# Down projection with stationary tokens, and a second filter step with products of 512: one change to a fused Hyena-filter and gated-MLP kernel

## The chip, the cores and the metric

The kernel runs on one core of one Trainium2 chip. The metric is the device time of one execution in microseconds (us). Engines are named as in the profile: PE is TensorE's matmul, PEld its weight load, DVE is VectorE, ACT is ScalarE, POOL is GpSimd.

## The reference

```python
# x, v: (4, 12480, 128); pos_emb: (12480, 64); w1: (64, 64); w2: (64, 128)
h_filt = (np.maximum(pos_emb @ w1, 0.0) @ w2) * np.exp(-0.01 * pos)[:, None]
u = x * v
L = 2 * S                                            # S = 12480
y = irfft(rfft(u, n=L, axis=1) * rfft(h_filt, n=L, axis=0), n=L, axis=1)[:, :S, :]
x2 = (x * y).reshape(B * S, D)                       # 49,920 tokens of 128
h = x2 @ w_in                                        # w_in: (128, 2048)
return (h * np.cos(h)) @ w_out                       # w_out: (2048, 128)
```

All of it is fp32.

## The kernel before

The long convolution is a Fourier transform in two steps, a product with the filter's transform, and an inverse in two steps, all as matmuls. The filter and batch 0 are transformed first; everything after that is the MLP with the convolution of the following batches fed into it in small pieces. The MLP takes the tokens in 98 tiles of up to 128 rows by 4 tokens (512 columns, one PSUM bank), and each tile has 16 steps, one per 128 hidden channels. A step is an up product, then k and f (which bring the argument of the cosine into the sine's range), the sine, the gate, and four steps later the down product. The down product kept the weights stationary, so its sums lay channel by token and were transposed back at the end of the tile:

```python
def moe_up(pool, n, c):
    ph = ps_h.tile([P, BANK], F32, name="ph")                  # 4 banks
    nc.tensor.matmul(ph[:, 0:m], w_in_sb[:, c * P:(c + 1) * P], ats[n][:, 0:m], ...)
    nc.scalar.activation(a[:, 0:m], ph[:, 0:m], AF.Identity, bias=quarter[:, 0:1], scale=INV_TWO_PI)
    nc.vector.tensor_scalar(out=k[:, 0:m], in0=a[:, 0:m], ...)              # k: round a
    nc.gpsimd.tensor_tensor(f[:, 0:m], a[:, 0:m], k[:, 0:m], op=ALU.subtract)
    # ... then in moe_act: cs = Sin(f) on ScalarE, gt = ph * cs on VectorE

def moe_down(n, c, gt):                                        # acc: 1 bank
    nc.tensor.matmul(accs[n][:, 0:m], w_out_sb[:, c, :], gt[:, 0:m],
                     start=(c == 0), stop=(c == NFC - 1))

def moe_evict(pool, n):
    nc.scalar.copy(out=ot[:, 0:m], in_=accs.pop(n)[:, 0:m])

def moe_back(pool, n, ot):
    for i in range(G):                                         # G = 4
        transpose(pt[0:m, i * D:(i + 1) * D], ot[:, i * m:(i + 1) * m], ident)
    nc.scalar.copy(out=ob[0:m, :, :].rearrange("p h n -> p (h n)"), in_=pt[0:m, :])
```

The second step of the transform is followed by the complex product with the filter. Each `yield` ends a turn: the program hands the engines back to the MLP there. A pair of rows has four turns in the time of 2.9 MLP steps, so a step is followed by one turn or by two.

```python
def f2_product(pool, ps, h, k1):
    for r, op in ((0, ALU.subtract), (1, ALU.add)):
        nc.vector.tensor_tensor(y[:, r], uu[:, 0], hh[:, r], op=ALU.mult)       # 256 columns
        yield
        nc.vector.tensor_tensor(t[:, r], uu[:, 1], hh[:, 1 - r], op=ALU.mult)   # 256 columns
        nc.gpsimd.tensor_tensor(y[:, r], y[:, r], t[:, r], op=op)
        yield
```

At the start, batch 0's x*v is made in 30 tiles of two halves, spread over two engines half by half, while the filter's two layers and its first step run:

```python
first_u = u_units(0, 3, slots[0:R, :, :, :],
                  lambda j, half: nc.vector if half and j % 3 and j < 18 else nc.gpsimd)
# the sums of a tile: add on GpSimd, subtract on VectorE
```

## Time and profile before

| | before |
|---|---|
| time, median of three runs | 3786.0 us (3785.1 to 3786.1) |
| first product of the second inverse step of batch 0 | 338.7 us |
| last down product starts | 3778.3 us |
| span of the profiled run | 3783.9 us |

The prediction below shows the stretches, TensorE's timeline and four groups of instructions.

The timeline of all engines at one change of tiles (start, duration, instruction, in brackets the idle time before it and its releaser):

```profile
1011.59 0.63 ACT L741 ACTIVATE cs<-f 128x512 f32<-128x512 f32 x1 [0.55 <-POOL f L736]
...
1012.13 0.57 ACT L758 COPY ot<-acc 128x512 f32<-128x512 f32 x1
...
1012.75 0.70 PE L752 MATMUL acc<-gt,w_out_sb 128*128 128x512 f32 x1 [0.28 <-ACT ot L758]
```

### The profile page before, as it was taken

The page shows a single profiled execution, that of the slowest core. Times are in us where ns is not written, and L with a number is a line of the kernel's source. Part 1 is how long each engine was busy: PE and PEld are TensorE (multiplying, and loading weights), DVE is VectorE, ACT ScalarE, POOL GpSimd, SP SyncE. Part 2 cuts the span into 40 slices and gives each one's busy share as a digit, 9 for nine tenths or more (in the row PEclk, how much of TensorE's full clock was granted, in tenths as well). Part 3 has the DMA queues.
Part 4 walks back from the last instruction along what each step waited for, and adds up shares of the span by engine and source line. Part 5 has one row for each costly group of instructions (what it writes and reads, how often), then busy time and mean ns, then how long its engine had stood idle before and what let it go on. Part 6 is the DMA issues. An engine that isn't in the chain of part 4 may idle for free.

```text
span 3783.9 us, 47244 instructions
## 1 busy us (share of the span) xinstructions
PE 3704.6 (98%) x13546; PEld 2108.5 (56%) x13546; DVE 2774.6 (73%) x5658; ACT 2525.1 (67%) x4683; POOL 2594.2 (69%) x2342
## 2 busy tenths in 40 slices
PE   8898999999999999999999999999999999999999
PEld 6777555655466555555565556555566544444444
DVE  8887887688866777788766786788765566666666
ACT  5756776766665557766655567666664677777777
POOL 7666886488854665688745664788644577777776
PEclk9999999999999999999999999999999999999999
DMA  6253542022202550122203540122105200000000
GB/s 166 70 178 100 151 148 60 16 72 78 75 18 66 177 162 27 32 78 77 60 18 109 173 127 18 52 78 76 41 12 167 87 20 21 17 20 20 17 22 14
DMA packets 209499, 276.14 MB, mean 73 GB/s; under 512 B 17111, under 2 KB 146535, under 8 KB 209111
## 3 DMA queue, kind: packets, MB, share of 16 engines
q1 hardware_dynamic: 209239, 273.12, 24.4%
q8 instruction: 109, 1.79, 0.2%
q14 instruction: 151, 1.24, 0.1%
HBM read 193.64 MB, written 79.42 MB: 72 GB/s over the span
## 4 chain that ended last, share of the span: by engine, by line
PE 84%; POOL 7%; DVE 4%; ACT 2%; issue 2%; DMA 1%; SPq 0%; POOLq 0%; DVEq 0%; ACTq 0%
PE ph L727 31%; PE acc L752 26%; PE cv L752 5%; PE cv L491 5%; PE cv L466 4%; POOL f L736 4%; PE cv L402 3%; PE cv L442 3%; PE ph L126 2%; PE ps L402 2%; PE ps L442 1%; DVE k L733 1%; POOL slots L461 1%; ACT cs L741 1%; POOL tm L295 1%
## 5 line engine op out<-in xcount | busy, mean ns | idle before, releaser
L736 POOL TENSOR_TENSOR f<-a,k 128x512 f32<-128x512 f32 (+1 forms) x1568 | 1988.6, 1268 | 1049.6 <-DVE k L733 1048.6
L727 PE MATMUL ph<-at,w_in_sb 128*128 128x512 f32 (+1 forms) x3136 | 1601.0, 592 | 5.3 <-DVE gt L743 4.7
L730 ACT ACTIVATE a<-ph,quarter 128x512 f32<-128x512 f32 (+1 forms) x1568 | 1073.3, 685 | 751.1 <-PE ph L727 742.1
L752 PE MATMUL acc<-gt,w_out_sb 128*128 128x512 f32 (+1 forms) x2688 | 1373.6, 592 | 10.4 <-ACT ot L758 9.9
L743 DVE TENSOR_TENSOR gt<-ph,cs 128x512 f32<-128x512 f32 (+1 forms) x1568 | 1077.8, 687 | 318.9 <-ACT cs L741 291.6
L733 DVE TENSOR_SCALAR k<-a 128x512 f32<-128x512 f32 (+1 forms) x1568 | 772.7, 493 | 619.0 <-ACT a L730 597.8
L741 ACT ACTIVATE cs<-f 128x512 f32<-128x512 f32 (+1 forms) x1568 | 980.5, 625 | 338.1 <-POOL f L736 335.5
L752 PEld LDWEIGHTS acc<-gt,w_out_sb 128*128 128x128 f32 x2688 | 505.6, 189 | 663.5 <-issue 619.3
L727 PEld LDWEIGHTS ph<-at,w_in_sb 128*128 128x128 f32 x3136 | 554.1, 190 | 338.3 <-issue 266.6
L461 POOL TENSOR_TENSOR slots<-slots,t 120x256 f32<-120x256 f32 x384 | 311.7, 818 | 60.6 <-DVE t L460 40.1
L491 PEld LDWEIGHTS cv<-slots,tm 96*104 96x104 f32 x1920 | 240.4, 170 | 109.8 <-issue 82.6
L491 PE MATMUL cv<-slots,tm 96*104 96x128 f32 x1920 | 254.7, 275 | 9.8 <-DVE tm L291 4.9
L752 PE MATMUL cv<-gt,w_out_sb 128*128 128x512 f32 (+1 forms) x448 | 224.5, 583 | 0.7 <-DVE gt L743 0.7
L466 PEld LDWEIGHTS cv<-cs,slots 120*96 120x96 f32 x1536 | 176.7, 167 | 67.6 <-issue 65.7
L466 PE MATMUL cv<-cs,slots 120*96 120x120 f32 x1536 | 183.1, 266 | 0.0
L442 PE MATMUL cv<-slots,w 124*120 124x256 f32 x576 | 173.0, 380 | 0.0
L442 PEld LDWEIGHTS cv<-slots,w 124*120 124x120 f32 x576 | 103.6, 184 | 123.8 <-issue 110.9
L402 PEld LDWEIGHTS cv<-c,slots 104*124 104x124 f32 x768 | 132.5, 192 | 71.2 <-issue 58.3
L402 PE MATMUL cv<-c,slots 104*124 104x192 f32 x768 | 151.2, 326 | 4.8 <-DVE gt L743 3.5
L752 PEld LDWEIGHTS cv<-gt,w_out_sb 128*128 128x128 f32 x448 | 84.9, 190 | 104.5 <-issue 99.5
L390 DVE TENSOR_TENSOR xt<-xt,vt 104x256 f32<-104x256 f32 x177 | 137.9, 787 | 0.0
L476 DVE TENSOR_TENSOR slots<-cv,other 96x240 f32<-96x240 f32 x384 | 133.7, 394 | 4.2 <-ACT other L474 4.2
(129 smaller groups left out, 2586.9 us busy)
## 6 DMA issues: line engine op xcount, KB each, us to landing
h<-hd SPq DMA_DIRECT2D x144, 240.0 KB
tm<-td SPq DMA_DIRECT2D x96, 312.0 KB
xt<-in_x_dram SPq DMA_DIRECT2D x120, 208.0 KB
vt<-in_v_dram SPq DMA_DIRECT2D x120, 208.0 KB
xs<-in_x_dram SPq DMA_DIRECT2D x120, 208.0 KB
zd<-zs SPq DMA_DIRECT2D x119, 208.0 KB
zb<-zd SPq DMA_DIRECT2D x96, 256.0 KB
w<-wd SPq DMA_DIRECT2D x144, 116.2 KB
```

Source lines behind the costliest of these rows:

```text
L402: nc.tensor.matmul(ps[0:KE, i * 2 * N1:(i + 1) * 2 * N1], u[:, b, 0:KE, i], c1[0:u.shape[0], :, :].rearrange("p r k -> p (r k)"), start=Tr ...
L442: nc.tensor.matmul(pi, w[:, i, :], parts[0:KE, :, k], start=True, stop=True)
L461: nc.gpsimd.tensor_tensor(y[:, r], y[:, r], t[:, r], op=op)
L466: nc.tensor.matmul(ps[0:N1, (i * 2 + r) * N2:(i * 2 + r + 1) * N2], parts[0:N2, r, :, b, i], cs[:, r, :], start=True, stop=True)
L491: nc.tensor.matmul(ps[0:R, i * D:(i + 1) * D], t[:, i, r, :], slots[0:N1, :, place, :], start=(r == 0), stop=(r == 1))
L727: nc.tensor.matmul(ph[:, 0:m], w_in_sb[:, c * P:(c + 1) * P], ats[n][:, 0:m], start=True, stop=True)
L730: nc.scalar.activation(a[:, 0:m], ph[:, 0:m], AF.Identity, bias=quarter[:, 0:1], scale=INV_TWO_PI)
L733: nc.vector.tensor_scalar(out=k[:, 0:m], in0=a[:, 0:m], scalar1=ROUND, scalar2=ROUND, op0=ALU.add, op1=ALU.subtract)
L736: nc.gpsimd.tensor_tensor(f[:, 0:m], a[:, 0:m], k[:, 0:m], op=ALU.subtract)
L741: nc.scalar.activation(cs[:, 0:m], f[:, 0:m], AF.Sin, scale=TWO_PI)
L743: nc.vector.tensor_tensor(gt[:, 0:m], ph[:, 0:m], cs[:, 0:m], op=ALU.mult)
L752: nc.tensor.matmul(accs[n][:, 0:m], w_out_sb[:, c, :], gt[:, 0:m], start=(c == 0), stop=(c == NFC - 1))
```

## The change

The intent was to take TensorE's 392 transposes back out of the path and with them one of ScalarE's two copies of each output tile, and to lighten VectorE. In the down projection the gated tokens become the stationary operand, so the sums come out with the tokens on the partitions and are stored as they are. In the second step VectorE makes two products of 512 columns where it made four of 256, with the filter kept in another order. The filter's results lie split by channels, so its first step needs three evictions per pair of channels instead of five and its second step products of 192 and 64 columns. Its hidden layer is written with one half mirrored, which makes the sums and differences of its output layer part of the matmul. And at the start whole tiles of x*v go to VectorE or to GpSimd, where halves did. Smaller parts of the same change, not shown in the diff below: two tables are loaded later, the filter's first step takes its channels in the opposite order, and the temporary tile of the products has two buffers instead of one.

```diff
 def moe_down(n, c, gt):
-    nc.tensor.matmul(accs[n][:, 0:m], w_out_sb[:, c, :], gt[:, 0:m],
-                     start=(c == 0), stop=(c == NFC - 1))
+    for i in range(G):
+        nc.tensor.matmul(accs[n][0:m, i * D:(i + 1) * D], gt[:, i * m:(i + 1) * m],
+                         w_out_sb[:, c, :], start=(c == 0 and i == 0),
+                         stop=(c == NFC - 1), skip_group_check=True)
 def moe_evict(pool, n):
-    nc.scalar.copy(out=ot[:, 0:m], in_=accs.pop(n)[:, 0:m])
-def moe_back(pool, n, ot):  ...            # four transposes and a second copy
+    nc.scalar.copy(out=ob[0:m, :, :].rearrange("p h n -> p (h n)"), in_=accs.pop(n)[0:m, :])

 def f2_product(pool, ps, h, k1):
+    for r, (dst, hh) in enumerate(((y, h[:, :, :, :]), (t[:, :, :, :], h[:, ::-1, :, :]))):
+        u = ...                                        # one of the two parts, read twice
+        nc.vector.tensor_tensor(dst, twice, hh, op=ALU.mult)              # 512 columns
+        yield
     for r, op in ((0, ALU.subtract), (1, ALU.add)):
-        nc.vector.tensor_tensor(y[:, r], uu[:, 0], hh[:, r], op=ALU.mult)
-        yield
-        nc.vector.tensor_tensor(t[:, r], uu[:, 1], hh[:, 1 - r], op=ALU.mult)
         nc.gpsimd.tensor_tensor(y[:, r], y[:, r], t[:, r], op=op)
         yield

 def filter_hidden(bank, aT, i, peT, w1_sb):
-    nc.scalar.activation(aT[:, 0:H, ...], pa..., AF.Relu)
+    nc.scalar.activation(to[0:FO], pj[0:FO], AF.Relu)
+    nc.scalar.activation(to[FO:P, ::-1, :], pj[FO:P], AF.Relu)
 # filter_out, f1_evict_filter, f2_mm(filt=True): the split by channels (cut)

-first_u = u_units(0, 3, slots[0:R, :, :, :],
-                  lambda j, half: nc.vector if half and j % 3 and j < 18 else nc.gpsimd)
+def taker(j):
+    dve = j >= 5 and (j % 2 == 1 if j < 19 else j % 3 == 2)
+    return nc.vector if dve else nc.gpsimd
+first_u = u_units(0, 3, slots[0:R, :, :, :], lambda j, half: taker(j),
+                  lambda j: (taker(j), taker(j)))
```

## The prediction

> **What bounds the kernel now.** I read the page's first rows, then the table by stretches, then the timeline of TensorE alone. The stretches first; their columns are busy microseconds of TensorE, its weight loads, VectorE, ScalarE, GpSimd, then the granted clock, DMA share and GB/s:
>
> ```profile
> 31.00:63.60 32.60, 26.12 (x121) 19.52 (x121) 29.95 (x83) 11.06 (x30) 27.33 (x32) 0.97 0.59 174
> 63.60:113.40 49.80, 47.05 (x256) 43.66 (x257) 46.48 (x155) 36.94 (x162) 43.12 (x77) 0.95 0.35 100
> 113.40:170.00 56.60, 45.18 (x258) 43.95 (x256) 44.88 (x126) 44.96 (x136) 35.01 (x44) 0.91 0.21 61
> 170.00:272.60 102.60, 96.26 (x480) 74.36 (x480) 92.98 (x288) 59.03 (x143) 67.22 (x96) 0.98 0.60 175
> 272.60:338.00 65.40, 56.15 (x512) 54.60 (x512) 49.52 (x153) 42.41 (x131) 45.16 (x60) 0.95 0.24 74
> 338.00:620.00 282.00, 266.91 (x1006) 150.59 (x1006) 231.38 (x384) 200.90 (x393) 232.91 (x211) 0.97 0.47 141
> 620.00:3000.00 2380.00, 2368.39 (x8857) 1353.70 (x8856) 1763.02 (x3538) 1504.96 (x2691) 1571.15 (x1360) 1.00 0.25 75
> 3000.00:3784.00 784.00, 778.71 (x1996) 358.13 (x1994) 498.02 (x887) 608.64 (x969) 558.85 (x443) 1.00 0.07 19
> ```
>
> The reader sees two kernels in one. From 620 us to the end (84% of the span) TensorE is busy over 99% of the time, the others 56 to 78%: a microsecond taken from VectorE or ScalarE there buys nothing, one taken from TensorE buys itself. Before 620 us nobody is full: engines take turns in holding each other up. The stretch 31 to 63.6 is the filter's output layer, then its first step, the first step of batch 0, the joint second step, the first inverse step, and 338 to 620 is the inverse of batch 0 beside the first 101 of the 1,568 up/down steps.
>
> Busy time of a matmul is not its cost, so I take the distance between starts from the timeline of TensorE:
>
> ```profile
> 2971.14 1.94 PE L491 MATMUL cv<-slots,tm 96*104 96x128 f32 x16
> 2972.92 1.02 PE L727 MATMUL ph<-at,w_in_sb 128*128 128x512 f32 x2
> 2973.78 1.02 PE L752 MATMUL acc<-gt,w_out_sb 128*128 128x512 f32 x2
> 2974.64 1.02 PE L727 MATMUL ph<-at,w_in_sb 128*128 128x512 f32 x2
> 2975.50 1.02 PE L752 MATMUL acc<-gt,w_out_sb 128*128 128x512 f32 x2
> 2976.36 0.60 PE L126 MATMUL ph<-ident,ot 128*128 128x128 f32 x4
> 2976.79 1.02 PE L727 MATMUL ph<-at,w_in_sb 128*128 128x512 f32 x2
> ```
>
> Two instructions of 512 columns take 0.86 us (429 ns each); sixteen of 128 columns 1.78 us (111 each), with 104-column weights loaded before each; four transposes 0.43 us (108 each). A product is two instructions.
>
> **What the Trainium skill says.** "TensorE: Matmul & The Clock Gate", Back-to-back issue gap: N/2.4 + 2.5 ns when warm. With each fp32 instruction passing its columns twice, this gives 512*2/2.4+2.5 = 429 and 128*2/2.4+2.5 = 109; the trace agrees. The same page, LDWEIGHTS: a load takes its columns/1.2 ns, 107 for 128, by columns alone. The trace shows 167 ns for 96 columns and 190 for 128, a slope of 0.7 ns a column over a constant, near the 0.83 of the page. "VectorE: DVE Perf Modes", The TRN2 errata: an fp32 tensor_tensor takes (N+151)/0.96 ns, so 424 for 256 and 691 for 512; the trace has 414 and 690. "PSUM — Partial Sum Buffer", The four PSUM rules: only the first matmul into a bank may carry the start flag and the others' columns are then overwritten, which is why the new down projection starts with its first quarter alone.
>
> **The change part by part.** *Down projection.* A step of two 512-column instructions becomes four products of 128 columns, eight instructions, each with its own load of 128 weight columns. If loads keep up: 8*109.3 = 874 ns against 858, so +16 ns. Steps after 620 us with whole tiles: 1,536 - 101 = 1,435, so +23.5 us. The last tile has 88 rows: it now streams 128 output channels four times whatever its rows, 874 against 2*296 = 592 ns, +4.5 us in 16 steps. It would rise on the path, all of it.
>
> *Transposes back.* Gone are four of 109 ns for each of 98 tiles, 90 of them after 620 us: -90*0.437 = -39 us, all on the path. Gone too is one of two ScalarE copies a tile:
>
> ```profile
> L767 ACT COPY ob<-ph 128x512 f32<-128x512 f32 x96 | 55.1, 574 | 2.9
> L758 ACT COPY ot<-acc 128x512 f32<-128x512 f32 x83 | 47.4, 571 | 0.0
> L458 DVE TENSOR_TENSOR slots<-cv,h 120x256 f32<-120x256 f32 x288 | 119.3, 414 | 0.0
> L743 DVE TENSOR_TENSOR gt<-ph,cs 128x512 f32<-128x512 f32 x1536 | 1060.1, 690 | 312.0 <-ACT cs L741 285.5 <-PE ph L727 11.2
> ```
>
> That is 55 us of ScalarE, hidden beside TensorE: nothing. At the very end one copy, the transposes and their latencies go: about -1 us.
>
> *Second step's products.* Four VectorE products of 256 (4*414 = 1,656 ns) become two of 512 (2*690 = 1,380), for 192 pairs of rows: 53 us of VectorE. 144 of them lie behind a full TensorE and are worth only some of the 31 us that TensorE loses there by waiting (sum of its start distances, 3,164 us, less the formula's): I put -3. The other 48 are the joint second step, which takes 102.6/48 = 2.14 us a pair, VectorE 91% busy. There VectorE falls from about 2.2 to 1.97 us a pair. But the filter's product, split by channels, goes from 256 columns (222 ns an instruction) to 192 and 64: about 166, and about 105, where the load of 120 weight columns sets the pace. TensorE then needs 4*222 + 4*(166+105) = 1.97 us a pair too, up from 1.78, and the stores already move 175 GB/s. Two engines at the same 1.97 don't interlock perfectly: about 2.07, so -3 us.
>
> *Filter.* Its output layer loses 60 VectorE sums of 411 ns (24.7 us) and gets 60 copies of about 370, 45 on ScalarE and 15 on VectorE; TensorE stays at about 26 us. VectorE was 92% busy in that stretch of 32.6 us: -5. The first step's eviction goes from five instructions per channel pair (1,561 ns on VectorE, 1,422 on ScalarE) to three (about 1,254 and 1,112), 38 of 64 on ScalarE: 42 and 33 us instead of 47 and 48. These stretches took 49.8 and 56.6 us where 256 instructions at 162 ns need 41.5, and ScalarE entered the second some 8 us behind. I take -9 over the two. GpSimd's work on x*v stays near 70 us (19 tiles of 3.7), so it bounds this gain. Two tables loaded later may cost the next stage +1.
>
> **Sum.** After 620: 23.5 + 4.5 - 39 - 3 - 1 = -15. Before: -5 - 9 - 3 + 1 = -16, in 338 to 620 about 0 (GpSimd as often the last as TensorE), and I allow +3 for waits I can't see. 3786 - 15 - 16 + 3 = **3758 us**, -0.7%.
>
> **Rivals.** (1) *Weight loads become the bound.* If a step's eight loads of 128 columns can't follow each other every 109 ns, say every 125, a step costs +142 ns and the kernel +205 us: about 3,960. For it: a load is shown at 190 ns, longer than the instruction it hides behind, the closest neighbour loads only 104 columns, and the page leaves 2 ns of margin. Against it: the transposes load 128 columns every 108 ns, the loads at 167 ns already follow each other every 111, and after the last transpose (2976.68) an ordinary 128-column load is followed by its product at 2976.79, 108 ns later. I give it 5%. A milder form, 111 instead of 109.3, costs +20 us: 3,778. (2) *The start of the kernel frees more than I think*, since the stretches to 338 us hold some 75 us of TensorE waiting: half of it gone would make 3,735. For it: VectorE and ScalarE lose work in every one of them. Against it: GpSimd's sums and the DMA queue at 175 GB/s aren't relieved. (3) *The transfers or the accumulator's single bank make a new wait*: the down projection still waits for ScalarE's copy at each tile (41 us of load waits at 45 places, but only 10 us of TensorE's). If the load can't be pulled ahead, since it now holds fresh data, some 0.3 us on 90 tiles make +27: 3,785.
>
> **Range and chances.** The middle is 3758. Faster starts give 3730, the mild load penalty with a wait 3790; I take 3732 to 3792. Over 2% faster means under 3,710, which needs TensorE work that the change does not remove: 0.05. Over 2% slower means over 3,862, reached only by rival 1 in full: 0.05. Within 2%: 0.90.
>
> **What would show it.** Starts of down instructions 109 to 111 ns apart, 0.87 to 0.89 us a step, and a tile of the last stage at 16*(0.858+0.875)+0.43 = 28.2 us against 28.4 now; no product from the transposes back; VectorE's new product at 690 ns, twice a pair; the joint second step at 2.05 us a pair; TensorE over 99% busy from about 605 us on. It would be wrong if down starts lie over 115 ns apart, if the 64-column products cost over 150 ns, or if the inverse of batch 0 starts before 305 or after 335 us (338 now).

## More of the kernel before

The page's part 4 says what the chain that ended last consists of, in shares of the span:

```profile
PE 84%; POOL 7%; DVE 4%; ACT 2%; issue 2%; DMA 1%; SPq 0%; POOLq 0%; DVEq 0%; ACTq 0%
```

TensorE carries 84% of the chain. The other engines together still hold 13%, though none of them is near full: there are places where TensorE hangs on a short chain through them.

Two rows of the waits (what waited, for what, us in total, times, longest) become important:

```profile
ACT cs L741 <- POOL f L736: 335.5, 885, 2.9
PE acc L752 <- ACT ot L758: 9.9, 15, 1.5
```

The sine waits for f on GpSimd in 885 of 1,568 steps. That costs nothing as long as TensorE is ahead. The second row is where it can cost something: the first down product of a tile needs the single accumulator bank, which ScalarE's copy of the tile before must have emptied.

## The result, and the profile after

| | before | after |
|---|---|---|
| time, median of four runs each | 3785.6 us (3782.8 to 3786.1) | 3813.6 us (3809.9 to 3817.1) |
| span of the profiled run | 3783.9 us | 3813.3 us |

The ratio is 1.0075, with a 95% interval of 1.0058 to 1.0093. A ratio here is always the mean time of one kernel's runs over that of the other's in the same rounds, so it is not quite the ratio of the medians quoted. The changed kernel is slower by 0.75%, where the prediction had 3758 us and a range of 3732 to 3792.

The stretches of the changed kernel, cut at the same events as those of before (the columns are those of the prediction's first fence, and the first row holds what came before the filter's output layer):

```profile
0.00:38.30 38.30, 21.64 (x66) 11.54 (x67) 18.28 (x42) 23.63 (x46) 17.97 (x32) 0.87 0.64 145
38.30:70.90 32.60, 28.57 (x241) 27.97 (x241) 17.01 (x39) 17.11 (x45) 16.13 (x22) 0.95 0.52 145
70.90:125.40 54.50, 47.99 (x256) 46.20 (x257) 39.48 (x95) 36.80 (x110) 38.88 (x72) 0.91 0.35 101
125.40:183.00 57.60, 45.81 (x258) 44.55 (x256) 42.59 (x116) 46.62 (x139) 36.30 (x48) 0.90 0.20 61
...
624.30:3050.00 2425.70, 2407.54 (x14831) 1882.77 (x14832) 1786.45 (x3283) 1487.42 (x2662) 1589.37 (x1378) 1.00 0.25 75
```

Rows three and four are the first steps of the filter and of batch 0. VectorE did get lighter there (39.5 and 42.6 us, for 46.5 and 44.9 before), ScalarE did not (36.8 and 46.6, for 36.9 and 45.0), and the stages got longer. From 624 us on TensorE is busy over 99% of the time, as it was. The second inverse step of batch 0 starts at 351.8 us instead of 338.7. From the starts of events in the two traces, the 29.4 us between the spans divide as follows.

| from | before | after | difference |
|---|---|---|---|
| start to the filter's output layer | 31.0 | 38.3 | +7.3 |
| output layer | 32.6 | 32.6 | 0.0 |
| filter, first step | 49.8 | 54.6 | +4.8 |
| batch 0, first step | 57.1 | 57.8 | +0.7 |
| joint second step and first inverse step | 168.2 | 168.5 | +0.3 |
| second inverse step of batch 0 | 276.5 | 272.5 | -4.0 |
| up to the last down product | 3163.1 | 3184.8 | +21.7 |
| tail | 5.6 | 4.2 | -1.4 |

So there are two losses: some 13 us at the start, and 22 us in the long stage where a gain of 15 had been expected. The distance between TensorE's starts in the last stage shows one part of the latter:

```profile
3300.96 1.05 PE L768 MATMUL cv<-w_out_sb,gt 128*128 128x128 f32 x8
3301.85 1.02 PE L740 MATMUL ph<-at,w_in_sb 128*128 128x512 f32 x2
3302.71 1.05 PE L768 MATMUL cv<-w_out_sb,gt 128*128 128x128 f32 x8
```

From the start of eight down instructions to the next instruction it is 0.89 us, 111 ns each, and not 109. The waits of the changed kernel:

```profile
ACT cs L754 <- POOL f L749: 399.6, 942, 2.9
...
DVE xt L395 <- DMA vt<-in_v_dram: 20.4, 8, 4.0
...
PE acc L768 <- ACT ob L775: 17.4, 25, 2.1
```

The sine waits 64 us more for f than before, and TensorE waits 17.4 us instead of 9.9 for the accumulator. The middle row is new: VectorE now waits for transfers of v, which before it never did (its x*v halves had no idle time ahead of them). Here is one late accumulator, at a place like the one shown of before:

```profile
1021.96 0.59 DVE L746 TENSOR_SCALAR k<-a 128x512 f32<-128x512 f32 x1 [0.34 <-ACT a L743]
...
1022.23 1.62 POOL L473 TENSOR_TENSOR slots<-slots,t 120x256 f32<-120x256 f32 x2
...
1023.57 0.68 DVE L470 TENSOR_TENSOR slots<-cv,h 120x512 f32<-120x512 f32 x1
1023.81 1.26 POOL L749 TENSOR_TENSOR f<-a,k 128x512 f32<-128x512 f32 x1
...
1024.17 1.20 DVE L746 TENSOR_SCALAR k<-a 128x512 f32<-128x512 f32 x1
...
1025.11 0.63 ACT L754 ACTIVATE cs<-f 128x512 f32<-128x512 f32 x1 [1.06 <-POOL f L749]
...
1025.65 0.57 ACT L775 COPY ob<-acc 128x512 f32<-128x512 f32 x1
...
1026.27 0.38 PE L768 MATMUL acc<-w_out_sb,gt 128*128 128x128 f32 x1 [0.76 <-ACT ob L775]
```

This is to be read from below. TensorE waited 0.76 us for ScalarE's copy, which ran directly after a sine, which had waited 1.06 us for f. The k of that f was done at 1022.55, but GpSimd was busy with two of the convolution's sums back to back (1.62 us), and f began at 1023.81. The harm goes on from there: the k of the next step stood behind a product of 512, began when that f was already running, and took 1.20 us, which makes the next f late. A k that meets no GpSimd instruction takes 427 ns in these traces.

The Trainium skill, "SBUF — State Buffer", section "Who interferes with whom", says why a k should be slow there: VectorE in a two-port mode (a tensor_scalar between fp32 tiles in SBUF can take one) and GpSimd share a pair of ports, whoever issues first holds it for its whole instruction, and the other is blocked, not slowed. The traces agree. A k of 512 columns takes 427 ns alone. That is less than the 552 that 512 columns would need at the tensor_tensor's pace (690 ns for 512 columns and 414 for 256, so 276 for 256 more), which fits a two-port mode. In the kernel after, past 640 us, a k that starts at least 0.05 us before the end of a running GpSimd instruction ends 284 ns after that end (median of 424; 281 to 358 ns for the middle nine tenths), wherever in it the k had started.

### The profile page after: what moved, and what is told of

It is laid out like the page before. It is cut to its first block, busy times and chain, and to the rows that moved or that the text cites.

```text
span 3813.3 us, 64967 instructions
## 1 busy us (share of the span) xinstructions
PE 3725.7 (98%) x22778; PEld 2918.9 (77%) x22778; DVE 2744.4 (72%) x5154; ACT 2484.2 (65%) x4564; POOL 2578.5 (68%) x2339
## 4 chain that ended last, share of the span: by engine, by line
PE 77%; POOL 10%; DVE 4%; DMA 3%; ACT 3%; issue 2%; SPq 0%; DVEq 0%; POOLq 0%; ACTq 0%
PE ph L740 29%; PE acc L768 26%; POOL f L749 6%; PE cv L768 5%; PE cv L503 5%; PE cv L478 4%; PE cv L407 3%; PE cv L454 2%; POOL slots L473 2%; DMA wd<-w 1%; DMA vt<-in_v_dram 1%; ACT cs L754 1%; PE ps L478 1%; DVE k L746 1%; DVE gt L756 1%
## 5 line engine op out<-in xcount | busy, mean ns | idle before, releaser
L768 PEld LDWEIGHTS acc<-w_out_sb,gt 128*128 128x128 f32 (+1 forms) x10752 | 1406.9, 191 | 670.2 <-issue 617.6
L768 PE MATMUL acc<-w_out_sb,gt 128*128 128x128 f32 (+1 forms) x10752 | 1420.6, 275 | 17.4 <-ACT ob L775 17.4
L746 DVE TENSOR_SCALAR k<-a 128x512 f32<-128x512 f32 (+1 forms) x1568 | 791.8, 505 | 661.7 <-ACT a L743 644.8
L754 ACT ACTIVATE cs<-f 128x512 f32<-128x512 f32 (+1 forms) x1568 | 980.8, 626 | 403.6 <-POOL f L749 399.6
L740 PEld LDWEIGHTS ph<-at,w_in_sb 128*128 128x128 f32 x3136 | 504.4, 191 | 29.3 <-DVE gt L756 8.1
L768 PEld LDWEIGHTS cv<-w_out_sb,gt 128*128 128x128 f32 (+1 forms) x1792 | 233.7, 189 | 102.2 <-issue 99.3
L503 PEld LDWEIGHTS cv<-slots,tm 96*104 96x104 f32 x1920 | 228.3, 170 | 12.1 <-DVE tm L296 5.1
L768 PE MATMUL cv<-w_out_sb,gt 128*128 128x128 f32 (+1 forms) x1792 | 235.3, 275 | 0.0
L395 DVE TENSOR_TENSOR xt<-xt,vt 104x256 f32<-104x256 f32 x187 | 142.9, 773 | 25.1 <-DMA vt<-in_v_dram 20.4
L407 PEld LDWEIGHTS cv<-c,slots 104*124 104x124 f32 x768 | 122.3, 193 | 5.4 <-POOL slots L401 3.8
L401 POOL TENSOR_TENSOR slots<-xt 104x256 f32<-104x256 f32 x128 | 110.5, 870 | 3.0 <-DVE xt L395 1.5
```

The source lines that it names most:

```text
L407: nc.tensor.matmul(ps[0:KE, i * 2 * N1:(i + 1) * 2 * N1], u[:, b, 0:KE, i], c1[0:u.shape[0], :, :].rearrange("p r k -> p (r k)"), start=Tr ...
L503: nc.tensor.matmul(ps[0:R, i * D:(i + 1) * D], t[:, i, r, :], slots[0:N1, :, place, :], start=(r == 0), stop=(r == 1))
L746: nc.vector.tensor_scalar(out=k[:, 0:m], in0=a[:, 0:m], scalar1=ROUND, scalar2=ROUND, op0=ALU.add, op1=ALU.subtract)
L754: nc.scalar.activation(cs[:, 0:m], f[:, 0:m], AF.Sin, scale=TWO_PI)
L768: nc.tensor.matmul(accs[n][0:m, i * D:(i + 1) * D], gt[:, i * m:(i + 1) * m], w_out_sb[:, c, :], start=(c == 0 and i == 0), stop=(c == NFC ...
```

## The experiments

There were fifteen runs. The ratio is to the kernel before in the same rounds (three or five of them), whose median was 3785.5 to 3787.7 us in each.

| label | what it is | median us | ratio (95%) |
|---|---|---|---|
| moe_only | before + new down projection | 3785.9 | 0.9996 (0.9982 to 1.0010) |
| conv_only | after, old down projection | 3813.1 | 1.0071 (1.0058 to 1.0083) |
| usplit | after, x*v split as before | 3801.9 | 1.0042 (1.0029 to 1.0054) |
| w96 | after, 96 stationary columns | 3795.2 | 1.0023 (1.0010 to 1.0037) |
| spread | after, GpSimd's sums apart | 3808.3 | 1.0058 (1.0044 to 1.0071) |
| halves | after, each 512 as two 256 | 3819.1 | 1.0086 (1.0072 to 1.0100) |
| acc2 | after, two accumulators | 3893.9 | 1.0284 (1.0270 to 1.0298) |
| best | usplit + spread + acc2 | 3885.0 | 1.0260 (1.0246 to 1.0274) |
| seq256_u | usplit + old order of products | 3782.6 | 0.9994 (0.9982 to 1.0007) |
| spread_u | usplit + spread | 3798.4 | 1.0027 (1.0013 to 1.0040) |
| spread256_u | spread_u, each 512 as two 256 | 3804.8 | 1.0048 (1.0035 to 1.0060) |
| turns256_u | usplit, one 256 a turn, sums a turn apart | 3798.7 | 1.0035 (1.0021 to 1.0049) |
| moe_acc2c | moe_only, 2nd accumulator from the convolution | 4177.0 | 1.1035 (1.1020 to 1.1050) |
| moe_acc2t | moe_only, 2nd accumulator from the up products | 3807.6 | 1.0060 (1.0046 to 1.0074) |
| best_c | usplit + spread, 2nd accumulator from the convolution | 4092.9 | 1.0814 (1.0799 to 1.0828) |

### The halves of the change, each alone

*Before with the new down projection only (moe_only):* `moe_down`, `moe_evict` and the main loop from the kernel after, everything else from the kernel before.

> The kernel before with the down projection of the change alone. Theory: the new down projection itself costs time, because its products follow each other every 111.6 ns and not 109, and because the first product of a tile waits longer for the eviction of the tile before. Then the start up to the first inverse product stays at 338.7 us, and the kernel takes 3800 to 3808 us, ratio 1.004 to 1.006. Rival: the loss is all of the start of the kernel (the changed convolution part) and the down projection gains as predicted: 3765 to 3775 us.

Neither theory held: the part is worth nothing, 0.9996. In its profile the parts can be told. After 640 us, by the prediction's formula, TensorE's instructions come to 3,093.9 us instead of 3,108.7. That is 14.8 us less, where the prediction's terms for the down projection and the transposes come to 11. The down instructions follow each other 111.25 ns apart instead of 109.2, and that gives back 20.6 us between them and another 3.5 behind the last one of each step. The waits of over 30 ns ahead of the first down product of a tile fall from 7.7 to 4.3 us. The sum of all start distances moves from 3,139.6 to 3,144.7 us; the profiled execution was the slowest of the five, 5 us above their median. The last stage, where TensorE waits for nothing, shows the steady cost: from the first up product of a tile to that of the next it is 28.46 us instead of 28.35, where the prediction had 28.2 against 28.4.

*After with the old down projection and its transposes (conv_only):*

> The changed kernel with the down projection and the transposes of before. Theory: the changed convolution part starts its first inverse product at 352 us as the changed kernel does, 13 us late, gets some 4 us back before 620 us and nothing after: 3792 to 3800 us, ratio 1.002 to 1.004. Rival (all of the loss is in the down projection, the late start is made up for later): 3780 to 3788 us.

3813.1 us: the whole loss is in the convolution's part (which here includes the filter and the start), far above what either theory gave it. The waits ahead of a tile's first down product were 17.8 us here, and 15.6 in the kernel after.

### The start

*x\*v split over halves as before (usplit):*

```diff
-def taker(j): ...
-first_u = u_units(0, 3, slots[...], lambda j, half: taker(j), lambda j: (taker(j), taker(j)))
+first_u = u_units(0, 3, slots[...],
+                  lambda j, half: nc.vector if half and j % 3 and j < 18 else nc.gpsimd)
```

> The changed kernel with the elementwise work on x*v of batch 0 divided over VectorE and GpSimd as before (halves of a tile), all else as changed. Theory: whole tiles on VectorE put its waits for the loads of v ahead of the evictions that it also makes, so the filter's first step starves of PSUM banks; undone, the waits of VectorE for loads (25 us) go, the filter's first step takes 44 to 48 us in place of 54.5, and the first inverse product starts at 338 to 345 us instead of 352: 3800 to 3808 us. Rival: the split is not the cause, the doubled ScalarE work of the hidden layer and the wait for loads are: first inverse product at 350 to 354 us, 3810 to 3816 us.

It gains 11.7 us, as the theory said, and the second inverse step of batch 0 starts at 338.9 us. Its filter's first step, in the table by stretches, and its wait:

```profile
64.70:113.00 48.30, 43.96 (x256) 41.47 (x257) 35.80 (x90) 37.05 (x111) 43.99 (x76) 1.00 0.37 111
```

```profile
DVE xt L395 <- DMA vt<-in_v_dram: 1.8, 6, 0.7
```

The stretch takes 48.3 us instead of 54.5 (just over the 44 to 48 expected), and VectorE's wait for v falls from 20.4 to 1.8 us. What happened there is visible in the timeline of the kernel after:

```profile
108.80 0.84 DVE L395 TENSOR_TENSOR xt<-xt,vt 104x256 f32<-104x256 f32 x2 [3.92 <-DMA vt<-in_v_dram]
...
110.46 0.55 DVE L442 COPY ftile<-ps 64x384 f32<-64x384 f32 x1
```

```profile
111.72 1.08 PE L407 MATMUL ps<-c,ftile 96*124 96x192 f32 x5 [2.60 <-DVE ftile L417]
```

VectorE stood 3.92 us at a tile of x*v whose transfer had not landed, with evictions behind it in its queue. TensorE then had no free bank, and waited 2.60 us for VectorE's eviction. In the split of before, GpSimd takes the first half of every tile, and it evicts nothing; by the time that VectorE comes to its half, v is there.

### The narrow stationary operand

*96 of the 128 stationary columns loaded (w96), which gives a wrong result (relative error 0.48):*

```diff
-nc.tensor.matmul(accs[n][0:m, i * D:(i + 1) * D], gt[:, i * m:(i + 1) * m], ...)
+mw = m if c == 0 else min(m, 96)
+nc.tensor.matmul(accs[n][0:mw, i * D:(i + 1) * D], gt[:, i * m:i * m + mw], ...)
```

> Wrong on purpose: the changed kernel whose down products load only 96 of 128 stationary columns (tokens) in all but the first product of a tile; the moving 128 columns, the instruction count and all else stay. Theory: the weight load of 128 columns is what spaces the products 111.6 ns; with 96 they follow each other every 109 ns, 2.4 ns less on 11,700 instructions after 620 us, so 26 to 30 us off: 3783 to 3789 us. Rival: the 2.4 ns come from the writes into the bank or from issue, not from the load: still 111 to 112 ns and 3810 to 3816 us.

```profile
3300.68 1.04 PE L769 MATMUL acc<-w_out_sb,gt 128*96 128x128 f32 x8
3301.55 1.02 PE L740 MATMUL ph<-at,w_in_sb 128*128 128x512 f32 x2
```

The eight now take 0.87 us. Over 9,422 such distances the mean is 109.1 ns, against 111.2 for full loads; the last tile of the kernel after, with 88 columns, has 109.2 over 116 distances. So it is the 128 stationary columns that make 111, and the instruction itself would allow 109. The edit narrows two things at once, the load and the partitions that are written, and no run separates them; but the transposes, which write 128 partitions, start 109.2 ns apart in the same trace (264 distances), which speaks for the load. The kernel gains 18.4 us by it; that is the size of the 20.6 us, and less than the 26 to 30 that I had expected.

### The products of the second step

*GpSimd's two sums kept apart (spread):*

```diff
     nc.vector.tensor_tensor(t, ...)                    # the second product of 512
+    sum(0)                                             # in the same turn
     yield
-    sum(0); yield; sum(1); yield
+    yield                                              # a turn without work
+    sum(1); yield
```

> The changed kernel with the same two VectorE products of 512, but GpSimd's first sum issued beside the second product and its second sum two turns later, as before the change. Theory: two sums of 0.81 us back to back on GpSimd hold up the step's own subtraction, ScalarE's sine behind it, and so the copy that empties the accumulator, so that the first down product of a tile waits; apart again, these waits after 640 us (15.6 us over, in 23 places, against 7.7 in the kernel before) fall to 6 to 9 us, and the kernel to 3802 to 3807 us. Rival (the length of VectorE's instruction, 690 against 414 ns, delays k and the sine): waits stay at 14 to 18 us, time at 3811 to 3816 us.

A part of it at most, and outside both ranges: 3808.3 us, 5 us less than the kernel after, though the two intervals overlap, and the waits ahead of a tile's first down product fall from 15.6 to 11.6 us and not to 6 to 9.

*Each product of 512 as two of 256 one behind the other (halves):*

```diff
-nc.vector.tensor_tensor(dst, twice, hh, op=ALU.mult)
+for q in range(2):
+    nc.vector.tensor_tensor(dst[:, q], u, hh[:, q], op=ALU.mult)
 yield
```

> The changed kernel with each product of 512 made as two of 256 (as before the change), the two GpSimd sums kept back to back at the end as in the change. Theory (bunched sums): the waits stay at 14 to 18 us and the time at 3811 to 3818 us, VectorE having 53 us more of work. Rival (instruction length): the waits fall to 6 to 9 us, 3802 to 3807 us.

3819.1 us, just above the first range and 5.5 us more than the kernel after, again with overlapping intervals. The waits stay (16.5 us in 24 places), so the length of the single instruction alone is not what makes them. It is no remedy in any case: shorter instructions in the same turn leave VectorE's piece of work per turn longer, 2*414 = 828 ns for 680.

*The old order: four products of 256 in four turns, each sum behind its own pair, and x\*v split as before (seq256_u):*

```diff
+for r, op in ((0, ALU.subtract), (1, ALU.add)):
+    nc.vector.tensor_tensor(y[:, r], u[0], h[:, r], op=ALU.mult); yield
+    nc.vector.tensor_tensor(t[:, r], u[1], h[:, 1 - r], op=ALU.mult)
+    nc.gpsimd.tensor_tensor(y[:, r], y[:, r], t[:, r], op=op); yield
```

> The changed kernel with two parts as before: x*v of batch 0 divided over both engines, and the second step's products as four of 256 with each GpSimd sum right behind its pair; the channel split, the layout of the stored filter, the filter layers and the new down projection stay as changed. Theory: the loss is these two parts alone; waits of first down products after 640 us fall to 4 to 8 us and the kernel to 3785 to 3792 us (the kernel with x*v alone restored took 3802). Rival: the layout or the lighter filter stages shift the phase of the steps, and some 7 us stay lost: 3795 to 3800 us.

3782.6 us (3782.2 to 3784.5), ratio 0.9994: level with the kernel before, with the whole of the new down projection, the new filter and its layout kept. These two edits therefore account for the loss, 11.7 us for the first (3813.6 to 3801.9) and 19.3 for the second on top of it (3801.9 to 3782.6); the second was not run without the first. The waits in its profile:

```profile
ACT cs L754 <- POOL f L749: 315.7, 924, 2.9
...
PE acc L768 <- ACT ob L775: 8.0, 11, 1.5
```

Against 399.6 us with 942 waits and 17.4 with 25 waits in the kernel after, both are back to the level of before.

*What of the order matters.* Three kernels, all with x*v split as before, take it apart: two products of 512 with the sums two turns apart (spread_u); the same with each 512 as two of 256 in one turn (spread256_u); and one product of 256 per turn with the sums one turn apart (turns256_u, order y0, y1, t0 with its sum, t1 with its sum).

> The changed kernel with x*v divided as before and the two GpSimd sums apart, products of 512. If spacing the sums is worth what it was in the other context: 3795 to 3798 us, waits of first down products after 640 us at 10 to 12 us.

> As the one before with each product of 512 made as two of 256 back to back in the same turn. Theory A (the order counts: with the first sum waiting for three of the four products, it and the step's own work on GpSimd still meet): 3794 to 3802 us, waits at 10 to 13 us. Theory B (the long instruction counts once the sums are apart): 3782 to 3787 us, waits at 4 to 6 us.

> The changed kernel with x*v divided as before and four products of 256, one in each of the four turns, in the new order (both products with the real part, then both with the imaginary part), so that the two GpSimd sums come in the last two turns, one turn apart. Theory (the length of VectorE's stretch in a turn delays k, which then finds GpSimd running and waits it out): 3782 to 3788 us, as the old sequence, k starting 0.15 to 0.20 us after the activation. Rival (the sums' distance counts as well): 3789 to 3797 us.

None of the three gets to 3783: spread_u lies at the edge of its range, spread256_u (3804.8 us) above both of its theories, and turns256_u (3798.7 us) above its theory and its rival. I took three figures from the records of each trace: the mean time from the start of a step's first activation to the start of its sine, in the second step of batches 1 to 3; what the k's lost to GpSimd after 640 us (their time over 427 ns where they met it); and the waits of more than 30 ns ahead of a tile's first down product, after 640 us, with their number.

| kernel | a to sine, us, batches 1, 2, 3 | k lost, us | first-down waits, us (number) | time, us |
|---|---|---|---|---|
| before | 3.12, 3.08, 3.15 | 93.9 | 7.7 (22) | 3785.6 |
| seq256_u | 3.09, 3.05, 3.14 | 81.0 | 3.9 (10) | 3782.6 |
| spread_u | 3.27, 3.28, 3.20 | 86.6 | 11.4 (20) | 3798.4 |
| turns256_u | 3.20, 3.30, 3.24 | 111.5 | 9.8 (23) | 3798.7 |
| usplit | 3.32, 3.39, 3.33 | 119.6 | 15.6 (23) | 3801.9 |
| spread256_u | 3.34, 3.40, 3.34 | 137.0 | 13.3 (23) | 3804.8 |

Among the five that differ in this order alone (all but before), the time from a to the sine, averaged over the three batches, is 3.09, 3.25, 3.25, 3.35 and 3.36 us, and the times of the kernels go with it: 3782.6, 3798.4, 3798.7, 3801.9 and 3804.8. Shorter products alone (turns256_u) and sums further apart alone (spread_u) each bring 3 us, which the intervals don't separate from nothing; both together, in the old order, bring 19, which they do. Why the two give together so much more than their sum is not settled. Where the 19 us lie can be read from TensorE's start distances: after 640 us its waits of over 30 ns come to 29.4 us in usplit and to 12.2 in seq256_u, 17.2 less. Of these, 11.7 lie ahead of first down products, 3.6 ahead of up products and 1.6 ahead of the other down products. Another 2.3 us are work that is already done at 640 us (3,091.2 us are left by the formula in usplit, 3,088.9 in seq256_u).

### A second accumulator bank

If TensorE waits for the one accumulator, a second should help. The program divides PSUM into eight banks: four for the up products, three for the convolution, one accumulator.

```diff
-ps_h bufs=4, ps_acc bufs=1          # acc2, best
+ps_h bufs=3, ps_acc bufs=2
-ps_c bufs=3, ps_acc bufs=1          # moe_acc2c, best_c; moe_acc2t: ps_h 3, tile transposes in ps_c
+ps_c bufs=2, ps_acc bufs=2
```

> The changed kernel with two accumulator banks, the second taken from the four of the up projection. Theory: the wait of a tile's first down product for the eviction of the tile before goes away whatever delays the eviction, 15.6 + 3.5 us after 640 us: 3793 to 3799 us. Rival: with three banks the up projection waits for VectorE's product instead, and the gain is under 5 us.

> The changed kernel with three of its parts mended: x*v of batch 0 divided as before, the sums apart, two accumulator banks. Theory: the start costs nothing (12 us off), the waits of first down products are gone (19 us off): 3780 to 3786 us, level with the kernel before, since the weight loads still space the down products by 111 ns. If the gains overlap less than I think, 3770 to 3780.

> The kernel before with the new down projection and with a second accumulator bank, taken from the three of the convolution. Theory: the wait of first down products (some 6 us there) goes and two banks are enough for the convolution, whose products come one pair a step: 3777 to 3783 us. Rival: with two banks the convolution waits for its evictions, over 3790 us.

> As the one before, but the second accumulator bank comes from the four of the up projection, and the transposes of the next tile go into a bank of the convolution instead. The kernel that took the bank from the up projection alone lost 80 us, 58 of it where the up projection follows those transposes. Theory: four uses of three banks were the loss, three in three are not: 3778 to 3786 us. Rival: three banks are too few for the up projection's chain even so: over 3800 us.

> The changed kernel with x*v divided as before, the two GpSimd sums apart, and the second accumulator bank taken from the convolution. Theory: start level with before, first down products no longer wait (11.6 + 3.3 us in the kernel with the sums apart): 3780 to 3786 us. Rival: the convolution misses the bank: over 3795 us.

All five failed. The waits of acc2 say why:

```profile
PE ph L740 <- DVE gt L756: 80.3, 93, 2.9
```

The waits for the accumulator were gone (0.8 us left ahead of first down products), and 80.3 us (4.7 in the kernel after) of waiting for an up bank had come in their place: the transposes of a tile use an up bank too, and three aren't enough at that moment. Taking the bank from the convolution was worse: in moe_acc2c its first inverse step alone waited over 120 us for its evictions. moe_acc2t, which moves the tile's transposes to the convolution's banks, still lost 0.6%. So the single accumulator is the cheapest of the ways tried to share eight banks, and its waits have to be kept away by the timing of ScalarE's copy. No version beat both kernels: seq256_u is level with the better.

## Why the prediction was right or wrong

The class held (within 2%), the range did not: the time is 22 us above its upper end. Three steps failed. The new down projection with its transposes, put at -11 us, came to about nothing (moe_only); the second step's products, put at -3 behind the full TensorE, cost 19 us (seq256_u against usplit); the start, put at -16, came to +13. Its own falsifier was met as well: "if the inverse of batch 0 starts before 305 or after 335 us". It started at 351.8.

**Right, by its steps.** "Gone are four of 109 ns for each of 98 tiles, 90 of them after 620 us: -90*0.437 = -39 us, all on the path", with +23.5 and +4.5 against it, makes -11: the sum by the formula fell by 14.8 us in moe_only. "VectorE's new product at 690 ns, twice a pair" came as 680 (the group's row is `L470`, below). The joint second step came at 2.07 us a pair, as predicted, partly by luck: its 64-column products cost less than assumed (below). The tail came at -1.4 for -1. The 55 us of ScalarE's copies were worth nothing.

**Mis-sized: "If loads keep up: 8*109.3".** They don't quite. The step was named with its remedy, "a milder form, 111 instead of 109.3, costs +20 us", and this is what came, 111.25 ns and 20.6 us (24 with the last instruction of each step). It should have been the main case: the prediction's own fence showed products with loads of 104 columns following each other every 111 ns. With the runs this lies in order for products of 128 columns: loads of 88 and 96 columns at 109, of 104 and 128 at 111. The evidence against it was read rightly but was of another kind. Transposes do load 128 columns every 109.2 ns, but such a load takes 141 ns in the trace, where one of a product takes 190; a load's time does not go by columns alone here, and the slope that the prediction drew through 167 and 190 ns hides it (104 columns took 167 ns too, 124 took 192).

**Wrong in sign: "144 of them lie behind a full TensorE ... I put -3".** Saved VectorE time behind a full TensorE was indeed worth nothing, but the step asked only how much VectorE works and not in which portions. The row of the new products reads

```profile
L470 DVE TENSOR_TENSOR t<-cv,h 120x512 f32<-120x512 f32 x144 | 98.0, 680 | 0.0
```

where the prediction's fence had 414 ns for 256. Each instruction holds up the k behind it for 0.27 us longer. GpSimd's sums come one turn apart, so that two can run back to back ahead of an f. A late f blocks the next k and delays its own sine, and at the end of a tile the copy that empties the accumulator stands behind that sine. This chain is read from the timeline; the runs show that the portions and their order cost 19 us, and do not separate the links. Rival 3 had the right place ("the down projection still waits for ScalarE's copy at each tile") and a wrong reason (a load that can't be pulled ahead); moe_only, which has the same fresh loads, waits less there than before.

**Wrong: "Before: -5 - 9 - 3 + 1 = -16".** It was +13. Three terms failed.
- *The output layer, -5.* usplit has 28.5 us for 32.6, so -4.1 was there to be had. But the kernel after lost it again by VectorE's waits for v, and the layer before it began late: "its output layer loses 60 VectorE sums" counted what the mirrored hidden layer saves and not what it costs. In the groups of the kernel after

```profile
L353 ACT ACTIVATE slots<-ps 64x480 f32<-64x480 f32 x11 | 6.2, 563 | 4.1 <-PE ps L350 4.0
L354 ACT ACTIVATE slots<-ps 64x480 f32<-64x480 f32 x11 | 6.2, 565 | 0.1
```

  two activations of 64 partitions stand for the one of 128 in the kernel before:

```profile
L345 ACT ACTIVATE slots<-ps 128x480 f32<-128x480 f32 x11 | 6.3, 572 | 3.8 <-PE ps L344 3.8
```

  That is 6.2 us more of ScalarE, and four copies that make the signed weights add 1.25 us. In usplit, where VectorE's waits are gone, the output layer still starts 5.2 us later than before; I put it down to this work, which no run tests alone.
- *The first steps, -9.* They gained 1.0 us in usplit (48.3 for 49.8 and 57.6 for 57.1). The evictions are lighter, but something else set the end. At the seam of the two stages TensorE waits once for an eviction that stands in ScalarE's queue behind rows of tables, and ScalarE waits for GpSimd to make these: 7.1 us before, 7.1 in usplit and 7.3 after. The line of usplit:

```profile
122.28 16.98 PE L407 MATMUL ps<-c,slots 104*124 104x192 f32 x85 [7.14 <-ACT ftile L415]
```

  GpSimd makes the last tables after its part of x*v, which ends at 96.5 us before and at 97.9 in usplit; the tables end at 119.8 and 120.8. The prediction's guard, "GpSimd's work on x*v stays near 70 us (19 tiles of 3.7), so it bounds this gain", looks like the answer (68.0 us before, 66.7 in usplit), though no run moves the tables, and it took 9 nevertheless. It did not ask what happens when an engine that evicts is given tiles that wait for transfers; that cost 11.7 us.
- *The joint second step, -3.* The new pace was right, the old one was not. Dividing the stretch by its pairs, 102.6/48 = 2.14 us, counted the stage's ends as pairs. From start to start of its 48 pairs the kernel before takes 2.06 us, so there was nothing to gain.

**Slips that changed little.** Rival 1's 3,960 counts the step's +16 ns twice: 142 ns a step stands against the old step and not against 3758, which already holds 23.5 us of it, so 3,939. "The others 56 to 78%" is 63 to 78% for VectorE, ScalarE and GpSimd in the two rows. The 64-column products, put at "about 105", came half at 55 to 57 ns and half at 104 to 107.

## What to carry to other kernels

Where a full engine depends on short chains through others, count not only what an engine works but also the pieces in its queue ahead of the chain and their order: here 53 us less work on VectorE, in longer pieces and another order, cost 19 us. Work that may wait for a transfer was better placed here on the engine that frees no buffers for others (11.7 us). And where a matmul's spacing and its weight load differ by 2% on paper, measure that very pair, at the width that is planned, before thousands of them are counted on.

## What the Trainium skill lacked or had wrong

- "TensorE: Matmul & The Clock Gate", LDWEIGHTS: by its figure, which goes by columns alone, a load of 128 columns (107 ns) hides behind an fp32 instruction of 128 moving columns (109 ns). Here such instructions of products start 111.25 ns apart with loads of 128 columns and 109.1 ns apart with 96 (88 columns: 109.2), and a load of 128 columns takes 190 ns for a product and 141 for a transpose. The page's section before that one does say that loads and products together set the spacing, but has no figure for fp32.
- "PSUM — Partial Sum Buffer", Specifications (TRN2): its table says that any non-contiguous access slows matmuls significantly. The changed second step writes PSUM in runs of two fp32 values, 8 bytes, with a stride: in batches 1 to 3 its instructions of 256 columns start 223.1 ns apart, where the contiguous ones of before did 222.5.
- No page says outright that a ScalarE activation over 64 partitions takes as long as one over 128: 564 against 572 ns for 480 columns.
- "SBUF — State Buffer", Who interferes with whom, has the blocking right but gives factors of slowdown and no delay: a blocked fp32 tensor_scalar of 512 columns ends 284 ns after GpSimd's instruction (median), and 427 ns after its own start where it meets none.
